# Efficient attention and a highway layer on one core: weight landing buffers, tanh to SBUF, a plain fp16 product, and a remade list of steps

## The chip, the cores and the metric

The kernel runs on one core of a Trainium2 chip. A core has a matrix engine (TensorE, in the profile PE, with its weight loads as PEld), a vector engine (VectorE, DVE), an activation engine (ScalarE, ACT), a general engine (GpSimd, POOL) and an engine that only issues DMAs and waits (SyncE, SP). Each engine works through its own instructions in order and waits for others by semaphores. SBUF is the working memory, PSUM the memory that matrix products are written to. The metric is the device time of one execution in microseconds, and lower is better.

## The reference

Two layers follow each other. The first is linear attention over batch 8, 8 heads, 576 positions and 64 channels:

```
q_s = exp(q) / sum over channels of exp(q)         (after subtracting a maximum)
k_s = exp(k) / sum over positions of exp(k)        (after subtracting a maximum)
kv  = k_s^T v           per batch and head, 64 x 64
attn = q_s kv           -> x, 4608 tokens x 512
```

The second is a highway layer over the 4608 tokens, with two 512 x 512 weights and one bias:

```
H = max(x w_h, 0);  T = sigmoid(x w_t + b_t);  out = T*H + (1 - T)*x
```

All inputs and the output are float32. Inside, the kernel works with fp16 operands and fp32 sums.

## The kernel before

The 4608 tokens are cut into 36 tiles of 128 tokens. For each pair of batches there are nine tiles: four of the first batch, four of the second, and one that holds the last 64 positions of both. Tile 35 is the last. Tiles 0 and 4 are worked in two halves of the heads.

Per batch, `ek` and `eq` take the exponentials of k and q on ACT, `vc` casts v to fp16 (on POOL, ACT or DVE, by a letter in the list of steps), `kv` multiplies k and v on PE, `kr` and `kn` (DVE) take the reciprocal of the sums and write the normalised block to `kvb`, `qt` turns q on PE through PSUM, and `qc` copies it back (DVE or ACT).

Per tile, PE computes `xu` (q times kv), DVE takes a reciprocal (`rs`) and writes the normalised x in fp16 (`x`). PE turns x (`xt`), DVE or ACT copies it out of PSUM (`xe`), and PE multiplies it by both weights: `mh` gives x w_h/2 - x/2 into a bank `gps`, `mt` gives x w_t onto the bias in a bank `tps`. The bias gets there by `bw`: a matmul on PE, or a copy of the finished bias rows `ball` by ACT. `th` takes tanh of half of `tps` (ACT), `dd` takes d = max(-x/2, gps) (DVE), `uu` makes u = (tanh + 1) d, and `oo` makes the output u + x. So the sigmoid is written with tanh, and T*(H - x) becomes (tanh + 1) times d.

There are two ways to u. In 28 of the 36 tiles (line 396), `th` writes back into `tps` and DVE reads PSUM to form (tanh + 1) d in one instruction. In 8 "lifted" tiles, `th` writes fp16 to SBUF (line 377), POOL forms d + x (`ee`, line 388) and tanh times d (`uu`, line 394), and `oo` adds these two. `oo` runs on POOL in all tiles but the last, where DVE does it in two halves.

The order of everything is written out by hand: the text `ORDER` is a list of some 700 steps, such as `xu_5_0` or `bw_7:A`, and each step issues its instructions at that place. Since every engine works in order, this list sets the order on each engine. `fill_n` issues n matmuls without use, which keep PE busy while it has nothing to do.

Loads of k, q, v and the weights and nearly all stores are issued by SP, in the order of the list; each of k, q and v has three landing buffers. The weights land in tiles of their own (`w32`) and are cast to fp16 by `wtc` and `whc`; `whd` subtracts half of an identity from the diagonal blocks of w_h. Two neighbouring tiles share one output buffer of 128 x 2 x 512 float32 (`oo` in the pool `op`, 3 buffers), which two stores of 64 rows each empty. The tiles without a mate, 8, 17, 26 and 31 to 35, have one of 128 x 512 (tag `o1`).

PSUM has two banks for `tps`, two for `gps`, and one place for turned x, which all tiles share.

The softmax here doesn't subtract the row's maximum and nothing guards it: scores larger than these inputs give would overflow.

## Time and profile before

The median of three timed runs is 126.34 us (126.02 to 127.27). The profiled execution has a span of 126.1 us, so what the profile shows stands 0.2 us below the median.

| | |
|---|---|
| span of the profiled execution | 126.1 us |
| median of the timed runs | 126.34 us |
| busy: PE, DVE, ACT, POOL | 112.1, 101.4, 92.8, 70.2 us |
| moved by DMA | 40.08 MB, on average 318 GB/s |
| DMA in the first three quarters of the span | 370 to 405 GB/s in nearly every slice |
| granted TensorE clock | 0.977 on average |
| instructions | 3549 |

A line of a group reads: source line, engine, operation, what it writes and reads with shapes, how often; then the busy time and the mean duration of one; then the time for which the engine was idle before these instructions and who ended it. Instructions that follow each other on DVE overlap by some 0.08 us, so that two 0.68 us passes take 1.28 us. A row of the timeline gives the start, the duration, the engine and the line. A row of windows gives each engine's busy time in a stretch.

### The profile page before, as it was taken

To read this page: it belongs to the slowest core of one execution; us is meant where nothing else is said; L and a number is where in the kernel's file an instruction comes from. 1 tells how busy PE (TensorE), PEld (TensorE's weight loads), DVE (VectorE), ACT (ScalarE), POOL (GpSimd) and SP (SyncE) were. 2 spreads that over 40 slices of the span, in tenths; PEclk is the share of its full clock that TensorE was granted. 3 is DMA by queue.
4 is the path that set the end of the run, shared out by engine and by line. 5 is a ranking of instruction groups with operands and counts; after the bars stand their busy time and mean duration, and the time that the engine had idled before them with its cause. 6 is when DMAs were issued, how large, how long until landed. Compare 5 with 4: busy or idle time off the path is not lost.

```text
span 126.1 us, 3549 instructions
## 1 busy us (share of the span) xinstructions
PE 112.1 (89%) x1415; PEld 68.6 (54%) x1415; DVE 101.4 (80%) x237; ACT 92.8 (74%) x144; POOL 70.2 (56%) x71
## 2 busy tenths in 40 slices
PE   5798979994999799999999999999899999999800
PEld 4485854543755365556564666557456656555400
DVE  5504769996868779999989899989889989999640
ACT  4098363995747999968959979999899996557500
POOL 5030000485304694785716769999974896786610
PEclk9999999999599999999999999999999999999996
DMA  4999999999999999999999999999987363733994
GB/s 110 376 386 373 383 385 377 387 378 387 391 394 400 396 385 300 376 394 396 405 393 391 402 404 397 393 400 394 393 324 229 86 166 83 144 70 80 222 237 127
DMA packets 20372, 40.08 MB, mean 318 GB/s; under 512 B 1282, under 2 KB 3586, under 8 KB 20356
## 3 DMA queue, kind: packets, MB, share of 16 engines
q1 hardware_dynamic: 20192, 39.72, 90.1%
q8 instruction: 11, 0.18, 0.6%
q10 hardware_dynamic: 164, 0.14, 0.4%
q14 instruction: 5, 0.04, 0.1%
HBM read 30.41 MB, written 9.44 MB: 316 GB/s over the span
## 4 chain that ended last, share of the span: by engine, by line
PE 36%; DMA 22%; DVE 12%; POOL 9%; ACT 7%; SPq 5%; issue 3%; DVEq 0%; POOLq 0%; ACTq 0%
PE gps L363 11%; DMA q<-in_q_dram 9%; PE tps L357 9%; DMA w32h<-in_moe_w_h_dram 7%; POOL o L412 6%; DMA out_dram<-o 5%; PE xu L312 5%; PE qps L286 4%; DVE u L396 4%; PE turned L334 3%; DVE d L383 2%; ACT qe L276 2%; ACT ek L232 2%; PE kv L248 2%; PE turned L168 2%
## 5 line engine op out<-in xcount | busy, mean ns | idle before, releaser
L412 POOL TENSOR_TENSOR o<-u,x 128x512 f32<-128x512 f16 x27 | 31.2, 1155 | 33.2 <-DVE u L396 32.7
L363 PE MATMUL gps<-w16h,xT 128*128 128x512 f16 x144 | 36.9, 384 | 0.0
L357 PE MATMUL tps<-w16t,xT 128*128 128x512 f16 (+1 forms) x148 | 36.8, 373 | 0.0
L327 DVE TENSOR_TENSOR x<-xu,rs 128x512 f16<-128x512 f32 (+1 forms) x38 | 24.9, 659 | 1.2
L383 DVE SCALAR_TENSOR_TENSOR d<-x,gps 128x512 f16<-128x512 f16 x36 | 24.3, 679 | 1.0 <-PE gps L363 0.8
L379 ACT ACTIVATE tps<-tps 128x512 f32<-128x512 f32 (+1 forms) x29 | 16.4, 568 | 11.0 <-PE tps L357 9.6
L276 ACT ACTIVATE qe<-q 128x1024 f16<-128x1024 f32 (+1 forms) x24 | 19.8, 845 | 3.0 <-DMA q<-in_q_dram 3.0
L396 DVE SCALAR_TENSOR_TENSOR u<-tps,d 128x512 f16<-128x512 f32 (+1 forms) x29 | 19.3, 669 | 3.1 <-POOL o L412 1.4
L357 PEld LDWEIGHTS <-xT 128*128 128x128 f16 x148 | 13.6, 98 | 11.6
L363 PEld LDWEIGHTS <-xT 128*128 128x128 f16 x144 | 13.2, 99 | 11.9 <-issue 0.5
L232 ACT ACTIVATE ek<-k 128x1152 f16<-128x1152 f32 (+1 forms) x20 | 18.8, 966 | 0.2 <-DMA k<-in_k_dram 0.2
L347 ACT COPY tps<-ball 128x512 f32<-128x512 f32 x27 | 15.9, 594 | 3.4 <-DVE u L396 3.4
L238 POOL CAST v<-v 128x1152 f16<-128x1152 f32 (+1 forms) x11 | 10.6, 969 | 10.8 <-DMA v<-in_v_dram 9.6
L312 PE MATMUL xu<-kvb,eq 128*128 128x130 f16 (+1 forms) x160 | 15.0, 229 | 1.4 <-DVE kvb L266 1.2
L334 PE MATMUL turned<-idh,x 128*128 128x128 f16 x144 | 14.4, 222 | 0.2 <-ACT xT L341 0.2
L168 PE MATMUL turned<-blank 128*128 128x256 f16 x88 | 12.4, 295 | 2.2 <-POOL blank L147 1.3
L312 PEld LDWEIGHTS <-eq 128*128 128x128 f16 (+1 forms) x160 | 10.3, 103 | 6.1 <-DVE kvb L266 1.7
L286 PE MATMUL qps<-idh,qe 128*128 128x128 f16 x144 | 12.3, 222 | 1.3 <-ACT qe L276 1.2
L334 PEld LDWEIGHTS <-x 128*128 128x128 f16 x144 | 9.8, 99 | 6.0 <-DVE x L327 2.7
L286 PEld LDWEIGHTS <-qe 128*128 128x128 f16 x144 | 9.5, 99 | 5.5 <-ACT qe L276 2.5
L168 PEld LDWEIGHTS <-blank 128*128 128x128 f16 x88 | 9.0, 106 | 4.1 <-POOL blank L147 1.3
L394 POOL TENSOR_TENSOR u<-th,d 128x512 f16<-128x512 f16 x8 | 9.2, 1155 | 2.8 <-ACT th L377 1.3
(45 smaller groups left out, 111.4 us busy)
## 6 DMA issues: line engine op xcount, KB each, us to landing
out_dram<-o SPq DMA_DIRECT2D x28, 256.0 KB, 9.6
v<-in_v_dram SPq DMA_DIRECT2D x6, 1152.0 KB, 13.5
k<-in_k_dram SPq DMA_DIRECT2D x6, 1152.0 KB, 13.9
q<-in_q_dram SPq DMA_DIRECT2D x6, 1152.0 KB, 14.0
k<-in_k_dram SPq DMA_DIRECT2D x4, 576.0 KB, 9.4
v<-in_v_dram SPq DMA_DIRECT2D x4, 576.0 KB, 6.6
out_dram<-o SPq DMA_DIRECT2D x14, 128.0 KB, 3.0
q<-in_q_dram SPq DMA_DIRECT2D x2, 640.0 KB, 11.4
```

Source lines behind the costliest of these rows:

```text
L168: nc.tensor.matmul(spare, blank[:, 0:P], blank[:, 0:2 * P], start=True, stop=True, skip_group_check=True)
L232: nc.scalar.activation(t[:, :, c:c + n].rearrange("p j c d -> p c j d"), T[f"k32{b}"][:, c:c + n].rearrange("p c (j d) -> p c j d", j=NJ), ...
L276: nc.scalar.activation(t[:, j0:j1].rearrange("p j c d -> p c j d"), T[f"q32{b}"].rearrange("p c (j d) -> p c j d", j=NJ)[:, :, j0:j1], AF.Exp)
L286: nc.tensor.matmul(t[:, (j - j0) // 2, 2 * kk:2 * kk + 2, (j - j0) % 2], T[f"qe{b}"][:, j, 2 * kk:2 * kk + 2].rearrange("p c d -> p (c d)" ...
L312: nc.tensor.matmul(dst, T[f"eq{b}_{jp // 2}"][:, jp % 2, n], kvb[b % NKV][:, hh, kk], start=True, stop=True, skip_group_check=True)
L327: nc.vector.tensor_mul(t[:, k0:k1], sums(i, k)[:, :, :, 0:64], T[f"rs{i}_{k}"][:, 0:k1 - k0].unsqueeze(3).to_broadcast([P, k1 - k0, 4, D]))
L334: nc.tensor.matmul(t[:, n], T[f"x{i}"][:, n * P:(n + 1) * P], idh, is_transpose=True, start=True, stop=True, skip_group_check=True)
L357: nc.tensor.matmul(T[f"tps{i}"][:, cs], T[f"xT{i}"][:, n], w16["t"][:, n, cs], start=False, stop=(n == 3), skip_group_check=True)
L363: nc.tensor.matmul(t, T[f"xT{i}"][:, n], w16["h"][:, n], start=(n == 0), stop=(n == 3), skip_group_check=True)
L383: nc.vector.scalar_tensor_tensor(t, T[f"x{i}"], -0.5, T[f"gps{i}"], op0=ALU.mult, op1=ALU.max)
L396: nc.vector.scalar_tensor_tensor(t[:, cs], T[f"tps{i}"][:, cs], 1.0, T[f"d{i}"][:, cs], op0=ALU.add, op1=ALU.mult)
L412: eng.tensor_add(t[:, cs], T[f"u{i}"][:, cs], T[f"{'e' if lifted(i) else 'x'}{i}"][:, cs])
```

## The change

- The tiles `w32` are gone. Each half of a weight lands in a buffer of the output pool, which now has seven buffers. One half of w_t is cast by ACT, the other by POOL, where DVE cast both.
- 33 tiles are lifted where 8 were. In these, tanh goes to SBUF as fp16 and u is a plain fp16 product of two SBUF tiles: on DVE in 16 tiles (`uu_..:T`), on POOL in 17 (`:P`). Of their 33 sums d + x, 12 are on DVE (`ee_..:D`) and 21 on POOL. Tiles 5, 28 and 35 still form u from PSUM.
- 10 of the output sums of whole tiles, and one half of the last tile's, are on DVE (`oo_..:D`), the rest on POOL, the last tile's other half among them.
- The last tile's two column halves have a PSUM bank each, the second from the pool of `qt`; its first product is of half 1, then half 0.
- The halves of tiles 0 and 4 may come in either order in `mt` and `mh`.
- A tile that holds rows of two batches, and the last one, is stored by one DMA where two were used. 13 stores are issued by ACT (`st_..:A`).
- The list of steps is new throughout: the order of loads (the weights come after q of batch 0), which copies are on which engine, where stores are issued, and 116 filling matmuls where 88 were.

Per engine the list moves these counts: copies of turned x on DVE from 22 to 17 and on ACT from 16 to 21; casts of v on ACT from 8 to 3, on DVE from 1 to 6, on POOL 11 as before; copies of turned q on ACT from 10 to 8; the bias by PE in 9 tiles before, in 8 and a half after.

```diff
--- before
+++ after
@@ ORDER @@
-b_0 b_32 setuppool fill_16 setupdve k_0_0 v_0_0 v_0_2 k_0_2 q_0_0 w_h_0 q_0_4 bsplit w_h_2 fill_4 bp w_t_0 bc vc_0_0:A
-w_t_2 bw_0:A ek_0_1 vc_0_2 k_1_0 ek_0_0 vc_0_3 vc_0_1:A ek_0_3 fill_30 kv_0_0 q_1_0 ek_0_2 kr_0_0 kn_0_0 fill_5 kv_0_1
-eq_0_0 v_1_0 kr_0_1 kn_0_1 fill_6 qt_0_0 whc_0 k_1_2 qc_0_0 half fill_9 xu_1_0 xu_0_1 xu_0_0 eq_0_1 rs_0_1 rs_1_0
-v_1_2 rs_0_0 x_1_0 bw_1:A x_0_0 fill_10 qt_0_1 x_0_1 whd_0 qc_0_1:A q_1_4 fill_2 xt_0_1 whc_2 xt_0_0 whd_1 whd_3
-xe_0_1 fill_6 xu_2_0 whd_2 xe_0_0 xt_1_0 rs_2_0 mh_0_0 v_2_0 xe_1_0 x_2_0 mh_0_1 eq_0_2 wtc_0:D mh_1_0 wtc_2:D mt_0_0
-dd_1 mt_0_1 dd_0 xu_3_0 th_0_0 xt_2_0 mt_1_0 rs_3_0 k_2_0 xe_2_0:D ek_1_0 uu_0_0 mh_2_0 th_1_0 x_3_0 eq_1_0 bw_2
...
-st_30_0_1 st_32_0_1 oo_33_0 th_34_0 mt_35_0 uu_34_0 st_33_0_0 mt_35_1 st_28_0_1 dd_35 th_35_0 oo_34_0 st_33_0_1
-th_35_1 uu_35_1 uu_35_0 st_34_0_0 oo_35_1 oo_35_0:P st_34_0_1 st_35_1_1 st_35_1_0 st_35_0_1 st_35_0_0
+setupdve v_0_2 k_0_0 q_0_0 k_0_2 b_0 ek_0_0 b_32 vc_0_3:A v_0_0 setuppool eq_0_0 ek_0_2 fill_20 bsplit vc_0_1:D ek_0_3
+q_0_4 w_t_0 fill_30 fill_30 half vc_0_2 vc_0_0 qt_0_0 w_h_0 ek_0_1 fill_20 kv_0_0 k_1_0 qc_0_0 w_t_2 kv_0_1 kr_0_0 w_h_2
+v_1_0 bp kn_0_0 eq_0_1 qt_0_1 q_1_0 xu_0_0 bc kr_0_1 kn_0_1 k_1_2 xu_0_1 wtc_0 rs_0_1 wtc_2:P xu_1_0 rs_1_0 qc_0_1:A
+rs_0_0 x_0_1 fill_16 v_1_2 whc_0 x_0_0 xt_0_1 x_1_0 vc_1_1 xe_0_1:D bw_0 whd_1 vc_1_0 xt_0_0 xe_0_0 xu_3_0 xt_1_0 rs_3_0
+xe_1_0 whd_0 bw_1 q_1_4 k_2_0 x_3_0 ek_1_1 whc_2 mt_0_0 xu_2_0 eq_0_2 mh_0_0 v_2_0 xt_3_0 mt_0_1 whd_2 rs_2_0 th_0_0
+mt_1_0 vc_1_2 q_2_0 whd_3 ek_1_0 mh_0_1 eq_1_0 th_1_0 xe_3_0:D mh_3_0 x_2_0 xt_2_0 kv_1_0 dd_0 kr_1_0 xe_2_0:D uu_0_0:T
+ek_1_2 dd_3 ek_1_3 vc_1_3:A mh_1_0 bw_2 mt_2_0 qt_1_0 dd_1 ee_0:D kn_1_0 oo_0_0:D bw_3 mh_2_0 th_2_0 kv_1_1 uu_1_0:P
+dd_2 kr_1_1 ee_3 mt_3_0 qc_1_0:A xu_4_0 eq_1_2 kn_1_1 qt_1_2 eq_1_1 ee_1:D qc_1_2 xu_5_0 th_3_0 rs_5_0 xu_4_1 bw_4
+qt_1_1 rs_4_0 x_5_0 qc_1_1 x_4_0 k_3_0 rs_4_1 xt_5_0 bw_5 qt_0_2 ee_2 xu_6_0 xe_5_0 x_4_1 xt_4_0 rs_6_0 v_3_0 ek_2_2
+uu_3_0:T x_6_0 mt_5_0 xt_4_1 oo_1_0 q_3_0 mh_5_0 xe_4_0:D xe_4_1:D xu_7_0 qc_0_2 rs_7_0 xt_6_0 mt_4_1 v_4_0 xe_6_0
+mt_4_0 oo_3_0 k_4_0 uu_2_0:T mh_4_1 th_5_0 mh_4_0 oo_2_0 vc_2_2 th_4_0 x_7_0 dd_5 vc_2_0:D ek_2_0 xu_8_0 bw_6 eq_2_0
+rs_8_0 xt_7_0 x_8_0 xe_7_0 dd_4 uu_5_0 mh_6_0 uu_4_0:P eq_2_1 kv_2_0 dd_6 mt_6_0 kr_2_0 th_6_0 qt_2_0 q_4_0 ee_4 mh_7_0
...
+xt_34_0 st_30_0_0 dd_33 uu_32_0:P bw_34:A oo_32_0 st_25_0_0:A ee_31:D oo_31_0 mt_33_0 xe_34_0 xt_35_0 st_32_0_1:A
+th_33_0 ee_33:D mh_34_0 uu_33_0:T mt_34_0 bw_35_0:A oo_33_0 dd_34 st_32_0_0 xe_35_0 ee_34:D mh_35_0 bw_35_1 th_34_0
+st_30_0_1 mt_35_1 st_28_0_0 st_31_0_0 st_31_0_1 st_23_0_0:A uu_34_0:T mt_35_0 st_33_0_0 dd_35 th_35_1 oo_34_0 st_33_0_1
+th_35_0 uu_35_1 st_34_0_1:A uu_35_0 oo_35_0:D st_34_0_0 oo_35_1 st_35_1_0 st_35_0_0:A
@@ -93,7 +94,7 @@
     xp = pool("xp", 6)
     xtp = pool("xtp", 3)
     dp = pool("dp", 3)
-    op = pool("op", 3)
+    op = pool("op", 7)
     PS = bass.MemoryType.PSUM
     ps_t = pool("ps_t", 2, space=PS)
     ps_g = pool("ps_g", 2, space=PS)
@@ -105,7 +106,6 @@
     idf = consts.tile([P, P], FP32, name="idf")
     idh = consts.tile([P, P], FP16, name="idh")
     half = consts.tile([P, P], FP32, name="half")
-    w32 = {w: consts.tile([P, KC, DM], FP32, name="w32" + w) for w in "th"}
     w16 = {w: consts.tile([P, KC, DM], FP16, name="w16" + w) for w in "th"}
     b32 = consts.tile([P, DM], FP32, name="b32")
     b16 = consts.tile([P, DM], FP16, name="b16")
@@ -139,8 +139,13 @@
     def halves(b, k):
         return (k, k + 1) if b < 2 else (0, 2)
 
+    PIECES = (0, 256, 512)
+
     def columns(i, h):
-        return slice(h * DM // 2, (h + 1) * DM // 2) if i == LAST else slice(0, DM)
+        return slice(PIECES[h], PIECES[h + 1]) if i == LAST else slice(0, DM)
+
+    def gate(i, h):
+        return f"tps{i}_{h}" if i == LAST else f"tps{i}"
 
 
     def setup_pool(e):
@@ -190,7 +195,8 @@
 
     def load_w(e, w, c):
         src = dict(t=moe_w_t, h=moe_w_h)[w]
-        nc.sync.dma_start(w32[w][:, c:c + 2], src.rearrange("(c p) n -> p c n", p=P)[:, c:c + 2])
+        T[f"w{w}{c}"] = op.tile([P, 2, DM], FP32, tag="o32", name=f"w32{w}_{c}")
+        nc.sync.dma_start(T[f"w{w}{c}"], src.rearrange("(c p) n -> p c n", p=P)[:, c:c + 2])
 
     def load_b(e, r):
         nc.scalar.dma_start(b32[r:r + 1], moe_b_t.rearrange("(o n) -> o n", o=1))
@@ -198,17 +204,18 @@
 
     def wt_cast(e, c):
         if e == "D":
-            nc.vector.tensor_scalar_mul(w16["t"][:, c:c + 2], w32["t"][:, c:c + 2], 1.0)
-        else:
-            nc.scalar.copy(w16["t"][:, c:c + 2], w32["t"][:, c:c + 2])
+            nc.vector.tensor_scalar_mul(w16["t"][:, c:c + 2], T[f"wt{c}"], 1.0)
+        else:
+            copy = nc.gpsimd.tensor_copy if e == "P" else nc.scalar.copy
+            copy(w16["t"][:, c:c + 2], T[f"wt{c}"])
 
     def wh_cast(e, c):
-        nc.vector.tensor_scalar_mul(w16["h"][:, c:c + 2], w32["h"][:, c:c + 2], 0.5)
+        nc.vector.tensor_scalar_mul(w16["h"][:, c:c + 2], T[f"wh{c}"], 0.5)
 
     def wh_diag(e, c):
         cs = slice(c * P, (c + 1) * P)
         nc.vector.scalar_tensor_tensor(
-            w16["h"][:, c, cs], w32["h"][:, c, cs], 0.5, half, op0=ALU.mult, op1=ALU.subtract)
+            w16["h"][:, c, cs], T[f"wh{c // 2 * 2}"][:, c % 2, cs], 0.5, half, op0=ALU.mult, op1=ALU.subtract)
 
     def bsplit(e):
         for r in (0, 32):
@@ -341,37 +348,43 @@
         copy(t[:, 2 * k0:2 * k1], T[f"xtps{i}"][:, 2 * k0:2 * k1])
 
 
-    def bw(e, i):
-        t = T[f"tps{i}"] = ps_t.tile([P, DM], FP32, tag="tps", name=f"tps_{i}")
+    def bw(e, i, h=0):
+        bank = (ps_t, "tps") if i < LAST or h == 0 else (ps_q, "qps")
+        t = T[gate(i, h)] = bank[0].tile([P, DM], FP32, tag=bank[1], name=f"tps_{i}_{h}")
+        cs = columns(i, h)
         if e == "A":
-            nc.scalar.copy(t, ball)
-        else:
-            nc.tensor.matmul(t, ones, b16, start=True, stop=False, skip_group_check=True)
+            nc.scalar.copy(t[:, cs], ball[:, cs])
+        else:
+            nc.tensor.matmul(t[:, cs], ones, b16[:, cs], start=True, stop=False, skip_group_check=True)
 
     def parts_of(i, k):
         return range(2 * k, 2 * k + 2) if i in HALVED else range(4)
 
     def mt(e, i, k):
         cs = columns(i, k)
-        for n in parts_of(i, k):
-            nc.tensor.matmul(T[f"tps{i}"][:, cs], T[f"xT{i}"][:, n], w16["t"][:, n, cs], start=False,
-                             stop=(n == 3), skip_group_check=True)
+        parts = parts_of(i, k)
+        first = once(f"mt{i}", lambda: k) == k and len(parts) < 4
+        for n in parts:
+            nc.tensor.matmul(T[gate(i, k)][:, cs], T[f"xT{i}"][:, n], w16["t"][:, n, cs], start=False,
+                             stop=(n == parts[-1] and not first), skip_group_check=True)
 
     def mh(e, i, k):
+        first = f"gps{i}" not in T
         t = once(f"gps{i}", lambda: ps_g.tile([P, DM], FP32, tag="gps", name=f"gps_{i}"))
-        for n in parts_of(i, k):
-            nc.tensor.matmul(t, T[f"xT{i}"][:, n], w16["h"][:, n], start=(n == 0), stop=(n == 3),
-                             skip_group_check=True)
-
-
-    LIFTED = {s.split(":")[0] for s in ORDER.split() if s.startswith("uu") and s.endswith(":P")}
+        parts = parts_of(i, k)
+        for n in parts:
+            nc.tensor.matmul(t, T[f"xT{i}"][:, n], w16["h"][:, n], start=(first and n == parts[0]),
+                             stop=(n == parts[-1] and not (first and len(parts) < 4)), skip_group_check=True)
+
+
+    LIFTED = {s.split(":")[0] for s in ORDER.split() if s.startswith("uu") and s[-2:] in (":P", ":T")}
 
     def lifted(i):
         return f"uu_{i}_0" in LIFTED
 
     def th(e, i, h):
         cs = columns(i, h)
-        src = T[f"tps{i}"][:, cs]
+        src = T[gate(i, h)][:, cs]
         if lifted(i):
             T[f"th{i}"] = dp.tile([P, DM], FP16, tag="th16", name=f"th16_{i}")
             nc.scalar.activation(T[f"th{i}"], src, AF.Tanh, scale=0.5)
@@ -385,15 +398,17 @@
     def ee(e, i):
         if lifted(i):
             T[f"e{i}"] = dp.tile([P, DM], FP16, tag="e16", name=f"e16_{i}")
-            nc.gpsimd.tensor_add(T[f"e{i}"], T[f"d{i}"], T[f"x{i}"])
+            eng = nc.vector if e == "D" else nc.gpsimd
+            eng.tensor_add(T[f"e{i}"], T[f"d{i}"], T[f"x{i}"])
 
     def uu(e, i, h):
         cs = columns(i, h)
         t = once(f"u{i}", lambda: dp.tile([P, DM], FP16, tag="u16", name=f"u16_{i}"))
         if lifted(i):
-            nc.gpsimd.tensor_mul(t, T[f"th{i}"], T[f"d{i}"])
-        else:
-            nc.vector.scalar_tensor_tensor(t[:, cs], T[f"tps{i}"][:, cs], 1.0, T[f"d{i}"][:, cs],
+            eng = nc.vector if e == "T" else nc.gpsimd
+            eng.tensor_mul(t, T[f"th{i}"], T[f"d{i}"])
+        else:
+            nc.vector.scalar_tensor_tensor(t[:, cs], T[gate(i, h)][:, cs], 1.0, T[f"d{i}"][:, cs],
                                            op0=ALU.add, op1=ALU.mult)
 
 
@@ -403,26 +418,27 @@
     def oo(e, i, h):
         cs = columns(i, h)
         if mate(i) is None:
-            t = once(f"o{i}", lambda: op.tile([P, DM], FP32, tag="o1", name=f"o32_{i}"))
+            t = once(f"o{i}", lambda: op.tile([P, DM], FP32, tag="o1", bufs=3, name=f"o32_{i}"))
         else:
             a = min(i, mate(i))
             both = once(f"oo{a}", lambda: op.tile([P, 2, DM], FP32, tag="o32", name=f"o32_{a}"))
             t = both[:, i - a]
-        eng = nc.vector if e == "D" or i == LAST else nc.gpsimd
+        eng = nc.vector if e == "D" else nc.gpsimd
         eng.tensor_add(t[:, cs], T[f"u{i}"][:, cs], T[f"{'e' if lifted(i) else 'x'}{i}"][:, cs])
 
     def st(e, i, h, r):
         bs, jp = tiles[i]
         b = bs[r % len(bs)]
         cs, rows = columns(i, h), slice(NP * r, NP * r + NP)
-        eng = nc.scalar if i == LAST and r else nc.sync
+        eng = nc.scalar if e == "A" else nc.sync
         dst = out[b * S:(b + 1) * S, cs].rearrange("(p j) n -> p j n", j=NJ)
         if mate(i) is not None:
             eng.dma_start(dst[:, 2 * jp + r - 2:2 * jp + r + 1:2], T[f"oo{i - 1}"][rows])
         elif len(bs) == 1:
             eng.dma_start(dst[:, 2 * jp + r], T[f"o{i}"][rows, cs])
         else:
-            eng.dma_start(dst[:, 8], T[f"o{i}"][rows, cs])
+            ends = out[b * S:(b + 2) * S, cs].rearrange("(r j) n -> r j n", j=NJ)
+            eng.dma_start(ends[:, 8], T[f"o{i}"][:, cs])
 
     does = dict(
         setuppool=setup_pool, setupdve=setup_dve, half=half_of_identity, bsplit=bsplit, fill=fill,
```

## The prediction

> **What bounds the kernel now.** I read the page first, then windows, waits, timeline and groups.
>
> ```profile
> span 126.1 us, 3549 instructions
> ...
> PE 112.1 (89%) x1415; PEld 68.6 (54%) x1415; DVE 101.4 (80%) x237; ACT 92.8 (74%) x144; POOL 70.2 (56%) x71
> ...
> L412 POOL TENSOR_TENSOR o<-u,x 128x512 f32<-128x512 f16 x27 | 31.2, 1155 | 33.2 <-DVE u L396 32.7
> ```
>
> PE is the busiest, and POOL alone has room. The page averages over stages, so I cut the span where the first matrix product of batch 1 starts (33.7) and where the products end.
>
> ```profile
> 0.00:18.00 18.00, 14.48 (x186) 11.14 (x187) 9.53 (x38) 9.82 (x14) 2.87 (x11) 1.00 0.93 333
> 18.00:33.70 15.70, 13.52 (x167) 8.33 (x166) 13.26 (x31) 10.83 (x18) 6.98 (x7) 0.93 1.06 383
> 33.70:119.30 85.60, 84.12 (x1067) 49.11 (x1064) 76.89 (x165) 71.42 (x111) 59.51 (x53) 0.99 0.90 313
> ```
>
> The columns after the length are PE, PEld, DVE, ACT and POOL. In the long stage PE is busy 84.1 of 85.6 us, and it is truly full: in the timeline four 512-column products follow each other at 0.86 us, 0.216 each, four of `xu` take 0.23 and four turns 0.22. A tile needs 8 x 0.216 + 0.23 + 0.22 + 0.22 and 0.16 of `kv`, 2.56 us; 32 tiles need 82 us. DVE is close behind with 76.9 (90%). Before this stage PE waits:
>
> ```profile
> 28.21 0.67 POOL L238 CAST v<-v 128x576 f16<-128x576 f32 x1
> ...
> 30.99 0.41 PE L312 MATMUL xu<-kvb,eq 128*128 128x130 f16 x4 [1.19 <-DVE kvb L266]
> ```
>
> The last product of tiles 0 to 3 starts at 27.4, the first of batch 1 at 33.7. POOL casts v at 28.21 because an output sum held it from 27.11; `kv` starts at 28.93 and DVE ends its four passes on the result at 30.94. The end is another chain:
>
> ```profile
> 118.18 1.04 PE L357 MATMUL tps<-w16t,xT 128*128 128x256 f16 x8
> ...
> 119.32 0.77 ACT L379 ACTIVATE tps<-tps 128x256 f32<-128x256 f32 x2 [1.21 <-PE tps L357]
> ...
> 122.36 1.20 SPq L425 DMA_DIRECT2D out_dram<-o  x2
> ```
>
> From 119.2 to the end are 6.9 us; SP issues stores without a pause from 116.2 to 123.6, 0.6 us each.
>
> **The head.** The order of loads changes, but v's second half of batch 1 stays the 15th load with the same bytes ahead; in the trace its neighbours land at 25.25 and 28.52, so it lands at about 26.9. POOL then has only casts in front: cast 26.9 to 27.6, `kv` to 28.2, `kr`, `kn` (0.17 + 0.59) to 29.0, `ee_1`, `qc_1_2` and reciprocals to 29.9, `x_5` to 30.5, turn and copy 0.8, product at 31.4 instead of 33.7: **2.3 us gained**. Behind POOL's early wait stand `uu_1` and sums, which PE doesn't need. w_h's second half moves from 15.9 to about 20.7 (one q and one k load more ahead at 1.5 us each, and part of w_t); tiles 0 to 3 then finish at about 28.3, still before 31.4, so it costs nothing unless it slips 3 us. The 28 more `fill` matmuls (0.11 us each, 3 us) end before w_t's second half can be cast at about 20.4: hidden. Casting w_t on ACT and POOL (1.05 each by the 1024-element rows) frees 1.3 us of DVE. The half clock in the middle row (0.93 of 15.7 us) I leave, as PE's pause has about the same length.
>
> **The tail.** Only one half is left after the last product: tanh 0.37, product 0.42, sum 0.42, one issue 0.6, landing 2.0 (from 123.0 to 125.0 before), closing 1.1: 5.0 with gaps, **1.9 us gained**. The other half's sum on POOL, about 0.6, lies beside it. Fewer stores (one DMA for two) and 13 issued by ACT take SP's row of issues away. On ACT they cost 13 x 0.6 = 8 us, and the instructions behind them wait: `xe_17`, `xe_34`, the last tanh. ACT loses five v casts (5.2) and gains five copies (2.9) and a weight cast (1.1), and so ends near 98 us: below PE.
>
> **Parts worth little.** The waits say so:
>
> ```profile
> ACT tps L347 <- DVE u L396: 3.4, 6, 0.8
> ...
> PEld L286 <- ACT qe L276: 2.5, 3, 1.3
> ...
> POOL o L412 <- DMA out_dram<-o: 0.4, 2, 0.2
> ```
>
> Tanh to SBUF frees the PSUM bank earlier, but only ACT waited for that, 3.4 us, and PE stayed full. Seven buffers replace three where POOL waited 0.4 us. Loads get ahead of stores, and PE waited under 1 us for the last q. Together 0 to 1 us.
>
> **DVE, passes counted.** A full 128x512 pass (0.68) costs 0.60 in a row, a copy of turned x 0.40. Gone: 25 u from PSUM (15.0), five copies (2.0), the weight casts (1.3), one half sum (0.3). Added: 10 full output sums (6.0), five v casts at 0.68 (3.4; the 1024-element cast row, 690 ns), and 28 products and sums of two fp16 SBUF tiles at a price p. That is -9.2 + 28p. No row shows p; the nearest are DVE's fp16 copy out of PSUM (mean 413 ns), its plain passes (0.68), and what POOL takes:
>
> ```profile
> L238 POOL CAST v<-v 128x1152 f16<-128x1152 f32 x7 | 8.0, 1143 | 4.7 <-DMA v<-in_v_dram 3.5 <-PE qps L286 1.2
> ...
> L238 POOL CAST v<-v 128x576 f16<-128x576 f32 x4 | 2.6, 664 | 6.1 <-DMA v<-in_v_dram 6.1
> ```
>
> Low end: the fp16 copy, 0.34 in a row; then DVE stays at its 101.4. Middle: the plain pass, 0.60; then 7 us more. High end: such a pass also waits for POOL. In this trace every pass that DVE runs beside POOL has at most one SBUF tensor of full size, and every pass with two (o, e, u) is on POOL or runs while POOL is idle. The change puts 28 + 10 with two SBUF tensors on DVE, beside a POOL that is busier still. POOL's rows say what it is short of: its casts cost 0.83 ns per column (1143 - 664 over 576), its two-tensor passes 1155 for 512, 1.9 ns per column after the same fixed part. [...]
>
> Price of that: POOL in the long stage has about 60 passes at 1.11 (their spacing at 74.66, 75.77, 76.88) and 6 casts, 74 us, some 80% of the stage. A DVE pass meets it with that chance and waits half a pass: 0.8 x 0.55 = 0.44. Of DVE's passes in the stage 25 fp16, 9 output sums and 5 casts are exposed: 39 x 0.44 = 17 us. By the same list DVE's stage is 76.9 us at p = 0.34, so 94; at 97% use (its best 6 us are 98%) 97 us from 31.0, and 5 us of tail: 133. From the other side, if the waits pack perfectly, POOL's 74 and the 17 us of DVE's exposed passes add to 91, from 31, and 4.5 after: 127. I take **130**.
>
> [...]
>
> **Rivals.** (1) *Nothing new is paid*, p = 0.34: PE decides, 31.4 + 82 + 2 us of its present waits + 5.0 = 120.5. For it: DVE at 76.9 of 84 is as full as now. Against it: two engines above 90% in fixed order. (2) *The plain pass*, p = 0.60: DVE's stage is 83.4, at 97% 86, from 31.0, then 5.0: 122.5. (3) *Waits half as long*: 39 x 0.2 gives DVE 84.7, 87.3, 31.0 and 5: 123.5 to 127, about no change. The turn between faster and slower lies at 0.27 us per exposed pass. (4) The list's stores on ACT or its new order stall PE where no buffer shows it: within 127.
>
> **How the numbers follow.** Span and timed median differ by 0.2 us; I leave that inside. Waits on POOL's reads (127 to 135, centre 130): 0.52. No price (119 to 122.5): 0.28. Plain pass (122 to 125): 0.12. Between (125 to 127.6, the 1% about 126.3 that a measurement of this kernel can hardly tell from no change): 0.08. So faster 0.40, same 0.08, slower 0.52; the likeliest case alone spans 127 to 135. The range for all runs from 120 to 133.5: it leaves out about 0.08 at either end.
>
> **What the next profile would show.** For my case: DVE rows of the fp16 product and of `ee` with means far above 0.42, or POOL passes above 1155; DVE above 93% in the long stage and PE with gaps in its products ended by DVE x or xT. Against it: these rows at 0.4 and POOL's still at 1155, PE as full as now. Head: first product of batch 1 at about 31.4. Tail: about 5 us from the last product to the end. I am wrong if DVE and POOL read side by side, or if the list keeps them apart.

## The result, and the profile after

The changed kernel takes 137.19 us (median of 4 runs, 136.74 to 137.51), the kernel before on the same chip 126.21 (126.02 to 127.27). The ratio is 1.0859, with a 95% interval from 1.0804 to 1.0914: the change makes the kernel 8.6% slower. The prediction was 130.0, slower, with a range of 120 to 133.5. Its side and its mechanism hold; its size does not.

The page of the changed kernel begins so:

```profile
span 135.1 us, 3623 instructions
...
PE 115.1 (85%) x1443; PEld 70.5 (52%) x1443; DVE 116.3 (86%) x249; ACT 93.5 (69%) x144; POOL 92.2 (68%) x85
...
DVE  5107589699999999999999999999999999999961
...
DVE 34%; POOL 12%; issue 7%; PE 5%; DMA 2%; SPq 1%; ACT 0%; DVEq 0%; POOLq 0%
```

DVE's row of slices stands at 9 from the ninth slice to the last but two, and in the chain that ended last DVE has 34% and PE 5%; in the kernel before it was DVE 12% and PE 36%. The bound has moved from PE to DVE. Cut at the same places as before (first product of batch 1, last product), with the columns PE, PEld, DVE, ACT and POOL:

```profile
18.00:35.17 17.17, 15.36 (x187) 9.13 (x186) 15.72 (x39) 10.58 (x19) 8.05 (x8) 1.00 1.06 383
35.17:127.51 92.34, 83.37 (x1058) 47.96 (x1057) 90.19 (x177) 73.72 (x115) 78.76 (x64) 1.00 0.85 283
127.51:135.10 7.59, 0.27 (x3) 0.00 (x0) 3.25 (x6) 0.61 (x2) 2.18 (x3) 0.77 0.69 190
```

Against the profiled execution of before, the head is 1.4 us longer (its first product of batch 1 came at 33.73), the long stage 7.1 (from 33.73 to 118.95 it was 85.2, with DVE at 76.5 and PE at 83.8) and the tail 0.4 (7.15). In the long stage DVE is now busy for 90.2 of 92.3 us, 98%; PE has 83.4 us of work, about as before, and waits the rest of the time. What it waits for is x:

```profile
PEld L341 <- DVE x L334: 6.3, 8, 1.7
PEld L319 <- DVE x L334: 5.2, 9, 1.2
...
PE turned L341 <- DVE x L334: 3.9, 4, 1.6
```

The first number is the sum of the waits, the last the longest. In the kernel before, the row of the turns (`PEld L334 <- DVE x L327`) stands at 2.7 us, the longest 0.5. Where DVE's time goes is seen in the groups, shapes kept apart:

```profile
L409 DVE TENSOR_TENSOR u<-th,d 128x512 f16<-128x512 f16 x16 | 12.4, 772 | 0.0
...
L402 DVE TENSOR_TENSOR e<-d,x 128x512 f16<-128x512 f16 x12 | 9.2, 772 | 0.2
...
L427 DVE TENSOR_TENSOR o<-u,e 128x512 f32<-128x512 f16 x8 | 7.5, 935 | 0.0
...
L245 DVE CAST v<-v 128x1152 f16<-128x1152 f32 x5 | 6.3, 1261 | 0.0
...
L396 DVE SCALAR_TENSOR_TENSOR d<-x,gps 128x512 f16<-128x512 f16 x36 | 24.1, 677 | 0.9 <-PE gps L376 0.5
```

The four kinds of pass that the change puts on DVE have means far above what the shortest of them take (about 0.4 for u and e); the pass `d`, with one operand in PSUM, has kept its 0.68. POOL's two-tensor rows went from about 1155 to 1202 (o), 1253 (e) and 1315 (u). In the timeline (start, duration, engine) each of these DVE passes starts 0.1 us behind one of POOL and ends only some 0.3 us after it:

```profile
118.98 1.16 POOL L427 TENSOR_TENSOR o<-u,e 128x512 f32<-128x512 f16 x1
119.08 1.34 DVE L409 TENSOR_TENSOR u<-th,d 128x512 f16<-128x512 f16 x1
120.22 1.21 POOL L409 TENSOR_TENSOR u<-th,d 128x512 f16<-128x512 f16 x1
120.34 1.37 DVE L402 TENSOR_TENSOR e<-d,x 128x512 f16<-128x512 f16 x1
```

The wait can be followed pass by pass. Of the 43 passes of these four kinds (16 u, 12 e, 10 o, 5 v), 28 start while POOL is in a two-tensor pass or a cast: they are longer than the pass alone (0.42, 0.42, 0.69 and 0.76 us, measured below) by 0.53 us in the mean and by at most 0.98. The other 15 are not longer at all.

A time stands 1.7 to 1.8 us above its execution's span in every run of this study. The executions of the kernel before are of two kinds, 125.2 to 126.4 us of span at a mean clock of 0.975 to 0.980 and 123.9 to 125.1 at 0.984 to 0.993, and the profiled one is of the first kind: its granted clock is 0.55 in the mean from 31.2 to 35.0 us, after PE's gap of 1.19 us. Where that stretch lies almost wholly ahead of the long stage or is missing, in two runs with the old list below, the stage takes 84.1 us; against that it has lost 8.3.

### The profile page after: what moved, and what is told of

Its sections match the earlier page's. It is cut to its first block, busy times and chain, and to the rows that moved or that the text cites. A ratio compares the mean times of both kernels' runs of the same rounds, so it can differ in the third digit from the quotient of the medians.

```text
span 135.1 us, 3623 instructions
## 1 busy us (share of the span) xinstructions
PE 115.1 (85%) x1443; PEld 70.5 (52%) x1443; DVE 116.3 (86%) x249; ACT 93.5 (69%) x144; POOL 92.2 (68%) x85
## 2 busy tenths in 40 slices
DMA packets 20293, 40.08 MB, mean 297 GB/s; under 512 B 1202, under 2 KB 3506, under 8 KB 20276
## 4 chain that ended last, share of the span: by engine, by line
DVE 34%; POOL 12%; issue 7%; PE 5%; DMA 2%; SPq 1%; ACT 0%; DVEq 0%; POOLq 0%
DVE x L334 9%; DVE d L396 6%; DVE u L409 4%; POOL o L427 4%; POOL e L402 3%; DVE e L402 3%; DVE o L427 3%; DVE v L245 3%; POOL u L409 3%; DMA out_dram<-o 2%; POOL v L245 2%; DVE eq L302 2%; DVE rs L328 2%; PE tps L368 1%; PE gps L376 1%
## 5 line engine op out<-in xcount | busy, mean ns | idle before, releaser
L427 POOL TENSOR_TENSOR o<-u,e 128x512 f32<-128x512 f16 x25 | 30.0, 1202 | 8.5 <-DVE u L409 4.7
L402 POOL TENSOR_TENSOR e<-d,x 128x512 f16<-128x512 f16 x21 | 26.3, 1253 | 5.8 <-DVE rz L267 3.3
L334 DVE TENSOR_TENSOR x<-xu,rs 128x512 f16<-128x512 f32 (+1 forms) x38 | 24.9, 658 | 0.7
L390 ACT ACTIVATE th<-tps 128x512 f16<-128x512 f32 x33 | 19.5, 595 | 6.4 <-PE tps L368 4.5
L409 POOL TENSOR_TENSOR u<-th,d 128x512 f16<-128x512 f16 x17 | 22.3, 1315 | 2.2 <-DVE d L396 1.2
L348 ACT COPY xT<-turned 128x512 f16<-128x512 f16 (+1 forms) x21 | 12.0, 574 | 15.5 <-PE turned L341 13.7
L245 POOL CAST v<-v 128x1152 f16<-128x1152 f32 (+1 forms) x11 | 12.0, 1092 | 13.1 <-DMA v<-in_v_dram 13.1
L173 PE MATMUL turned<-blank 128*128 128x256 f16 x116 | 15.1, 296 | 1.3 <-POOL blank L152 1.3
L356 ACT COPY tps<-ball 128x512 f32<-128x512 f32 (+1 forms) x28 | 15.9, 586 | 0.3
L319 PEld LDWEIGHTS <-eq 128*128 128x128 f16 (+1 forms) x160 | 9.6, 100 | 9.6 <-DVE x L334 5.2
L173 PEld LDWEIGHTS <-blank 128*128 128x128 f16 x116 | 12.2, 106 | 3.5 <-POOL blank L152 1.3
```

Of the source, the lines that this page charges most:

```text
L173: nc.tensor.matmul(spare, blank[:, 0:P], blank[:, 0:2 * P], start=True, stop=True, skip_group_check=True)
L319: nc.tensor.matmul(dst, T[f"eq{b}_{jp // 2}"][:, jp % 2, n], kvb[b % NKV][:, hh, kk], start=True, stop=True, skip_group_check=True)
L334: nc.vector.tensor_mul(t[:, k0:k1], sums(i, k)[:, :, :, 0:64], T[f"rs{i}_{k}"][:, 0:k1 - k0].unsqueeze(3).to_broadcast([P, k1 - k0, 4, D]))
L390: nc.scalar.activation(T[f"th{i}"], src, AF.Tanh, scale=0.5)
L402: eng.tensor_add(T[f"e{i}"], T[f"d{i}"], T[f"x{i}"])
L409: eng.tensor_mul(t, T[f"th{i}"], T[f"d{i}"])
```

## Experiments

**Theory.** A DVE pass that reads two tensors from SBUF and a POOL pass exclude each other. The new passes wait for POOL, this fills DVE, and a full DVE lets PE wait for x. **Rivals.** The number of passes on DVE, at any price; the new list of steps by itself; the weights in the output buffers; the late loads and the fills for the head; the stores for the tail.

The runs were taken in three groups, each with the kernel before beside it (medians 126.45, 127.26 and 126.37 us); a ratio is to the kernel before of its own group.

### The price by itself

Not the kernel, but rows of passes, each kind alone and then two kinds side by side:

```diff
+PHASES = [
+    ("product", 12, "", 0), ("sum32", 12, "", 0), ("onepsum", 12, "", 0), ("psumcopy", 12, "", 0), ("cast", 6, "", 0),
+    ("", 0, "sum", 8), ("", 0, "sum32", 8), ("", 0, "cast", 8),
+    ("product", 12, "sum", 12), ("sum32", 12, "sum", 12), ("onepsum", 16, "sum", 10), ("psumcopy", 24, "sum", 10),
+    ("cast", 8, "sum", 8), ("product", 10, "cast", 10)]
```

> Not the kernel at all (nothing of the reference is computed): rows of passes on DVE and POOL, each kind alone and then side by side. Theory: alone the fp16 product of two SBUF tiles takes 0.41, the sum with fp32 output 0.65, the pass with one operand in PSUM 0.68, the fp16 copy out of PSUM 0.41; POOL's sum 1.15. Side by side, the product and the sum with two SBUF tiles take turns with POOL's passes, so that a pair lasts 1.4 to 1.6 us from start to start and the DVE row's mean is above 1; the passes with an operand in PSUM stay as alone, and so does POOL beside them. [...] Rival, shared bandwidth: both kinds get longer together by a common factor, also those with a PSUM operand. Rival, no contention: all rows as alone.

The groups of this run, window by window: first alone (product, sum with fp32 output, pass with a PSUM operand, copy out of PSUM, cast; then POOL's sum), then side by side (products, sums, passes with a PSUM operand between POOL's row and the casts).

```profile
L61 DVE TENSOR_TENSOR u<-th,d 128x512 f16<-128x512 f16 x11 | 4.7, 425 | 0.4
L62 DVE TENSOR_TENSOR o<-th,d 128x512 f32<-128x512 f16 x11 | 7.6, 693 | 0.4
L63 DVE SCALAR_TENSOR_TENSOR dx<-x,g 128x512 f16<-128x512 f16 x11 | 7.6, 686 | 0.4
L79 DVE CAST v<-v 128x1152 f16<-128x1152 f32 x1 | 0.8, 759 | 0.6 <-DMA v<-in_v_dram 0.6
L68 POOL TENSOR_TENSOR p<-pa,x 128x512 f32<-128x512 f16 x8 | 9.2, 1150 | 0.5
...
L61 DVE TENSOR_TENSOR u<-th,d 128x512 f16<-128x512 f16 x12 | 15.1, 1256 | 0.4
L62 DVE TENSOR_TENSOR o<-th,d 128x512 f32<-128x512 f16 x12 | 18.3, 1523 | 0.4
L67 POOL TENSOR_TENSOR e<-pa,x 128x512 f16<-128x512 f16 x10 | 11.5, 1151 | 0.7
L63 DVE SCALAR_TENSOR_TENSOR dx<-x,g 128x512 f16<-128x512 f16 x16 | 11.0, 686 | 0.5
L65 DVE CAST v<-v 128x1152 f16<-128x1152 f32 x8 | 12.7, 1592 | 0.2
```

Beside POOL the product takes 1.26 us instead of 0.43, the sum 1.52 instead of 0.69, and the cast from SBUF to SBUF, which has one source, 1.59 instead of 0.76. The pass with one operand in PSUM stays at 0.686, and POOL beside it at 1.151; the copy out of PSUM stays at 0.42 too. So it is turns and not shared bandwidth, and the cast of v belongs to those who pay. In each of the three the excess is the same 0.83, though their own times differ.

### The 38 passes without what they read: a failed try

In the changed kernel the 16 products, the 12 sums `e` and the 10 output sums on DVE become copies of an unused block in PSUM.

```diff
+    still = turned[:, 1].rearrange("p c d -> p (c d)")
...
-            eng.tensor_mul(t, T[f"th{i}"], T[f"d{i}"])
+            if e == "T":
+                nc.vector.tensor_copy(t, still)
+            else:
+                nc.gpsimd.tensor_mul(t, T[f"th{i}"], T[f"d{i}"])
```

> The changed kernel, in which DVE's 16 fp16 products u, its 12 sums e and its 10 full output sums are each replaced by one copy of an unused 128x512 fp16 block in PSUM into the same destination (those products and sums are left out; POOL's part, all loads, stores and matrix products stay). The nearest row is the copy of turned x out of PSUM, 406 ns, which kept that time beside POOL. Theory (a DVE pass with two SBUF tensors and a POOL pass exclude each other): the 38 passes lose some 12.5 us of waiting, DVE in the long stage falls from 90.2 to about 78, POOL's sums go back to about 1.16, PE decides again, and the span falls from 135.1 to 126 to 129 us (the head and the tail keep their losses), timed 128 to 130.5. Rival, that the number of DVE passes and their places in the list make the loss, and not what they read: the same number of passes in the same places, so 134 to 137.

136.98 us (136.59 to 137.06), ratio to the kernel before 1.0802 (1.0743 to 1.0861): the time of the changed kernel, as the rival had it. But the groups and the waits say something else:

```profile
L412 DVE COPY u<-turned 128x512 f16<-128x512 f16 x16 | 6.7, 417 | 2.7 <-PE turned L342 1.8 <-ACT xT L349 0.8
...
L405 POOL TENSOR_TENSOR e<-d,x 128x512 f16<-128x512 f16 x21 | 24.2, 1155 | 7.9 <-DVE d L397 7.7
```

```profile
ACT xT L349 <- DVE e L403: 6.6, 3, 2.3
...
PE turned L342 <- DVE o L432: 1.7, 4, 0.6
```

The price is gone (417 ns, POOL's `e` at 1155 again), and DVE's long stage fell to 80.6 us of a stage of 94.2. But the unused block lies in the tile `turned`, into which PE turns x, and the semaphores now order PE's turns, ACT's copies and DVE's copies among each other. The experiment put a new wait in the place of the old one and settles nothing about the time.

### The same with fills

The same 38 passes become fills with a constant, which read nothing. A fill takes 485 ns, so 38 cost 18.4 us; what they replace would cost 28 x 0.42 + 10 x 0.69 = 18.7 if it did not wait.

```diff
-            eng.tensor_mul(t, T[f"th{i}"], T[f"d{i}"])
+            if e == "T":
+                nc.vector.memset(t, 0.25)
+            else:
+                nc.gpsimd.tensor_mul(t, T[f"th{i}"], T[f"d{i}"])
```

> The changed kernel again with its 38 DVE passes over two SBUF tensors left out (16 products u, 12 sums e, 10 output sums), but now each is a fill of the same destination with a constant, which reads nothing and so brings no new dependence; in the copies out of PSUM it was seen that PE's turns of x and these copies waited for each other, since they lie in one PSUM tile. A fill of 128x512 took 485 ns, fp16 or fp32, in the rows of passes measured alone. Theory (waiting for POOL): DVE's long stage falls from 90.2 to about 78, PE is busy all through it, the stage lasts 85 to 87.5 us where it took 92.3, span 128 to 130.5, timed 129.5 to 132.5. Rival, that the new list holds PE up by itself, whatever DVE's passes cost: the stage stays above 90, timed 135 to 137. A fill that waits for POOL too would show as a row mean above 0.55; then the run says little.

129.85 us (129.15 to 131.17), ratio 1.021 (1.0104 to 1.0316). Its groups and its long stage:

```profile
L404 POOL TENSOR_TENSOR e<-d,x 128x512 f16<-128x512 f16 x21 | 24.3, 1155 | 4.0 <-DVE rz L267 3.0 <-DVE d L396 0.9
...
L411 DVE MEMSET u<- 128x512 f16 x16 | 7.8, 485 | 0.9
...
L245 DVE CAST v<-v 128x1152 f16<-128x1152 f32 x5 | 5.4, 1071 | 0.0
```

```profile
34.94:119.36 84.42, 83.34 (x1059) 48.17 (x1057) 79.84 (x179) 73.19 (x115) 74.39 (x64) 1.00 0.91 309
```

The time and DVE's stage are as expected, the stage a little shorter. It goes from 92.3 to 84.4 us, PE is busy for 83.3 of it, and DVE falls to 79.8. The places in the list, the number of passes and their price alone are the same as in the changed kernel; what is taken away is reading, and with it the waiting (the fills also drop their waits for tanh and d, but in the changed kernel DVE idled 0.0 and 0.2 us ahead of these groups). So the waits make nearly the stage's whole loss: 84.4 us stand against 84.1 with the old list, and the new list by itself costs the stage next to nothing. What is left of the 2.1% is the head (its first product of batch 1 comes at 34.94) and the tail (8.0 us).

### The old list in the changed code, and 24 such passes in it

`old_list` keeps of the change the seven buffers with the weights in them, the last tile's two banks and the single stores; the order, the lifted tiles and the engines are those of the kernel before.

> The changed kernel's code with the list of steps of the kernel before (28 tiles with u out of PSUM, all output sums on POOL, no store on ACT), so that of the change there remain the seven output buffers in which the weights land, the last tile's halves in banks of their own with half 1 first and half 0's sum on DVE and the other's on POOL, and one store where a tile holds rows of two batches. Theory: nothing of this costs anything; the tail gains 1 to 2 us and the long stage stays at 85 us, so 124 to 126 us against 126.2. Rival, that the weights in the output pool or the banks cost something: 127 or more, with PE waiting in the head for weights.

125.92 us (125.65 to 127.19), ratio 0.9955 (0.9913 to 0.9998): at the upper end of what was expected, half a percent at most. The long stage is 84.1 us and the tail 6.8. Buffers, banks and stores cost nothing, and bring little.

`old_list_24` adds to it, in 12 tiles, one product and one sum of two SBUF tensors on DVE, with POOL's passes as they were:

```diff
-uu_7_0
+uu_7_0:T ee_7:D
 (the same for tiles 10, 12, 13, 16, 18, 19, 23, 24, 25, 27 and 29)
```

> The same as old_list, but in 12 tiles of the middle (7, 10, 12, 13, 16, 18, 19, 23, 24, 25, 27, 29) tanh goes to SBUF, and DVE makes u as a product of two fp16 SBUF tiles and e as their sum with x, in the place where it made u out of PSUM; POOL's passes stay the same in number. Alone, a tile costs DVE 2 x 0.41 - 0.60 = 0.2 more, 2.6 in all. Theory: each of the 24 passes waits 0.38 in the mean, 9 us, so DVE's long stage rises from 76.5 to about 88 of then 89 us, the rows of both have means near 0.75, and the time is 3 to 6 us above old_list. Rival, no waiting: rows at 0.41, DVE at 79 of 85, within 0.7 us of old_list, or faster since the bank of tps comes free earlier.

129.84 us (129.29 to 130.91), ratio 1.0255 (1.0181 to 1.033), 3.9 above `old_list`. Its groups:

```profile
L409 DVE TENSOR_TENSOR u<-th,d 128x512 f16<-128x512 f16 x12 | 7.5, 624 | 1.0 <-ACT th L390 0.9
L402 DVE TENSOR_TENSOR e<-d,x 128x512 f16<-128x512 f16 x12 | 6.9, 574 | 0.0
```

The loss is in the expected window, and the rival's rows at 0.41 are not there. But the means are 0.62 and 0.57 where 0.75 was expected: 4.3 us of waiting instead of 9. POOL is busy here for 59.3 of 87.9 us, where it was 78.8 of 92.3. But its busy share is not the chance of a meeting: 8 of the 24 passes start during a pass of POOL, and those wait 0.54 in the mean, the others not at all. Where the list places a pass decides whether it pays. DVE stands at 81.0 of 87.9 and not at its limit, so the time also goes to waits of x in the fixed order: PE's weight loads wait 5.3 us for x ahead of a turn, against 2.4 in `old_list`.

### Giving the passes back: two tries

In `no_two_sbuf` the 16 tiles form u from PSUM again, POOL takes over the output sums and the four sums `e` of DVE that are left, and ACT the casts.

```diff
-uu_3_0:T ... ee_10:D ... oo_5_0:D ... vc_2_0:D
+uu_3_0 (ahead of the bias that takes its bank) ... oo_5_0 ... vc_2_0:A
```

> The changed kernel with these parts undone, everything else as it is: the 16 tiles whose u was a fp16 product on DVE form u from PSUM again (their sums e fall away, and where the next bias needs the bank, u stands before it), the other 4 sums e of DVE and its 9 whole output sums in the remaining places go to POOL, and 5 casts of v go from DVE to ACT. So DVE has no pass with two SBUF tensors but the last tile's half. Theory: DVE's stage falls from 90.2 to about 76 us, POOL's stays near 78, and the stage comes to 85 to 88 us: span 127 to 131, timed 129 to 133. Rival, the list: 135 or more, with PE waiting for other things than DVE's x.

138.11 us (137.52 to 138.71), ratio 1.0863 (1.0765 to 1.0962). DVE is down to 70.7 of 93.3 us and POOL's rows are at 1155 to 1158, but now the bank decides:

```profile
ACT tps L356 <- DVE u L411: 7.9, 7, 2.2
...
DVE u L411 <- ACT tps L392: 6.8, 7, 2.5
```

In the second try the bias is moved behind u instead, and 4 of the tiles form u on POOL.

> A second try at the changed kernel without DVE passes over two SBUF tensors, since in the first try u was moved up in the list and DVE then waited for tanh, and ACT's next bias for u: now 12 of the 16 tiles form u from PSUM in the place where u stands, with the bias of the tile that takes the bank moved behind it; the other 4 form u on POOL; the remaining sums e and the output sums of DVE are on POOL and the 5 casts of v on ACT, as before. DVE's stage then needs some 72 us and POOL's some 83. Theory: 129 to 133, since no engine is above 90%. Rival (the new list needs the bank to be free right after tanh): ACT waits for u and PE for the bias, 134 to 138, as in the first try.

141.72 us (140.7 to 142.63), ratio 1.1188 (1.111 to 1.1266): worse. DVE waits for tanh 7.0 us, ACT for u 7.7, and POOL, now at 87.2 of 99.9 us, is late with a cast of v that the product of k and v waits for. Both misses say the same: the new list is built on a bank that is free right after tanh, and its DVE passes could not be taken back in these two ways. They say nothing about the price.

### The head

`head_old` has the first part of the old list, up to the last step of kv of batch 1, and then the new one.

> The changed kernel with the first part of the old list, up to the last normalising of kv of batch 1 (loads, fills, casts, tiles 0 to 3 with u out of PSUM), and the rest of the new list as it stands. Theory: the head's loss comes from the new list's first part alone (bias load late behind an exponential on ACT, 116 fills, casts of the weights beside POOL), so the first product of batch 1 comes at 33 to 34.5 instead of 35.2, and the time falls by 0.7 to 2.2, to 135 to 136.5. Rival, that the long stage swallows it (it is bound by DVE's passes, which are the same): no change within 0.5.

135.34 us (135.3 to 135.65), ratio 1.0666 (1.059 to 1.0743): 1.85 below the changed kernel's median, and 1.2 in the profiled spans (133.9 and 135.1). The first product of batch 1 comes at 33.72, and the long stage, 92.5 us with DVE at 89.9, is the same. The head's loss stands by itself and adds to the stage's.

`fewer_fills` takes 36 fills out of the new head, and `b_and_fills` puts the bias loads first as well.

```diff
-b_0 ek_0_0 b_32 ... ek_0_1 fill_20 kv_0_0 ... x_0_1 fill_16 v_1_2
+(b_0 b_32 first, in b_and_fills alone) ... ek_0_1 kv_0_0 ... x_0_1 v_1_2
```

> The changed kernel without two of its rows of fills: the 20 that stand on PE ahead of the first product of k and v, and the 16 ahead of the first turn of x. In its trace the 20 end at 14.79, while the two casts of v that this product needs end at 12.0 and 13.3, and the 16 run from 17.58 to 19.49 where the first x is ready at 18.5. Theory (the head's loss is made by PE's fills): the first product of k and v comes at 13.4 instead of 14.7, the first x is turned a microsecond earlier, the first product with a weight stands at 20 or earlier (21.4), and the first of batch 1 comes 0.5 to 1.4 us earlier than 35.2; timed 135.7 to 136.7. Rival, the weights: the second half of w_t is cast at 20 to 21 whatever PE does, and nothing is gained after it: within 0.4 of 137.2. A half clock after the missing fills would eat the gain; the granted clock tells.

> The same as fewer_fills, and in addition the two loads of the bias stand first on ACT's queue, as in the kernel before, so that DVE no longer waits 7.1 us for them with a cast of v behind. Theory: that cast ends near 11.5 instead of 13.3, the first product of k and v starts at 12.2, when PE has ended its earlier fills and turns, and the head gains another 0.5 to 1 us over fewer_fills: first product of batch 1 at 33.2 to 34.2, timed 134.8 to 136. Rival, that v's load of batch 1 sets the head (it lands at 27 in either kernel): nothing beyond fewer_fills.

In the timeline of the changed kernel the bias holds DVE until 12.5 with a cast of v behind it, and the fills hold PE until 14.8, so that the first product of k and v starts at 14.71:

```profile
11.05 0.42 DVE L222 CAST b<-b 1x512 f16<-1x512 f32 x1 [7.09 <-DMA b<-in_moe_b_t_dram]
...
12.44 2.35 PE L173 MATMUL turned<-blank 128*128 128x256 f16 x20
12.57 0.75 DVE L245 CAST v<-v 128x576 f16<-128x576 f32 x1
...
14.71 0.78 PE L255 MATMUL kv<-v,ek 64*64 64x65 f16 x72
```

Without the fills it starts at 12.27, but the first product of batch 1 gains only 0.5 (34.66); with the bias first as well it comes at 34.01. The times are 136.24 (135.94 to 136.78; ratio 1.0759, 1.0687 to 1.083) and 136.51 (135.73 to 137.49; 1.0783, 1.0713 to 1.0852). The second kernel's time misses its window, as three of its four runs have a granted clock of 0.968 to 0.975 against 0.985 in the best one, which took 135.73. Taking fills and late bias away gives back 1.16 of the head's 1.4 us. How much of it is the bias is not shown: with the bias first, the first product of k and v comes at 13.39 and not at the expected 12.2, while in `fewer_fills` PE waits 0.81 and 2.00 us ahead of its turns of x and behind that works at about half the speed: two products of 512 columns take 1.06 us at 20.32 where they take 0.59 in `b_and_fills`, whose granted clock is 1.00 from 18 to 34 us (in the mean of the profiled executions 0.974 and 0.985). So the fills that were in the way may also have kept the clock up.

The rest stands behind kv, and there the head pays the stage's price. In the changed kernel the sum `e` of tile 1 lies between the normalised kv and x of batch 1:

```profile
31.19 0.59 DVE L273 TENSOR_TENSOR kvb<-kv,rz 64x128 f16<-64x128 f32 x2
31.82 0.95 DVE L402 TENSOR_TENSOR e<-d,x 128x512 f16<-128x512 f16 x1
```

From the start of that normalising to the start of x it takes 2.05 us (x at 33.24). In `head_old`, which has no such sum there, it takes 1.39 (30.36 to 31.75). That is 0.66 of the 1.45 us between the two heads.

### The tail

> The changed kernel with six buffers instead of three for the output of tiles without a mate, so that tile 35's sums don't wait until tile 32's store has landed. Theory: both sums of the last tile start as soon as u is there, 1.2 to 1.4 us earlier; the stores then wait for nothing but SP and ACT issuing them; timed 1 to 1.8 us less than 137.2. Rival, that the stores' queue sets the end: the last store is issued after the others anyway, and the gain is under 0.4.

```diff
-t = once(f"o{i}", lambda: op.tile([P, DM], FP32, tag="o1", bufs=3, name=f"o32_{i}"))
+t = once(f"o{i}", lambda: op.tile([P, DM], FP32, tag="o1", bufs=6, name=f"o32_{i}"))
```

137.73 us (137.01 to 137.95), ratio 1.0839 (1.0755 to 1.0923): no gain. Changed kernel, then this one, each with the last tile's sums and last store:

```profile
131.16 0.67 POOL L427 TENSOR_TENSOR o<-u,x 128x256 f32<-128x256 f16 x1 [1.38 <-DMA out_dram<-o]
131.19 0.92 DVE L427 TENSOR_TENSOR o<-u,x 128x256 f32<-128x256 f16 x1 [1.21 <-DMA out_dram<-o]
...
132.14 0.38 ACTq L441 DMA_DIRECT2D out_dram<-o  x1
```

```profile
130.37 0.67 POOL L427 TENSOR_TENSOR o<-u,x 128x256 f32<-128x256 f16 x1
...
130.65 0.66 DVE L427 TENSOR_TENSOR o<-u,x 128x256 f32<-128x256 f16 x1
...
131.53 0.52 SPq L441 DMA_DIRECT2D out_dram<-o  x1
```

The waits are gone and the sums run 1.2 to 1.4 us earlier (from the last product, which is 0.63 later here). But from the last issue to the end it takes 135.9 - 132.05 = 3.85 us where it took 135.1 - 132.52 = 2.58: SP's six stores of 128 KB, the last store at 131.53 among them, land after 3.3 us in the median, where the one issued at 132.14 landed after 1.9. The DMA rows of the last 10 us, 0.25 us per digit, of the changed kernel and of this one, suggest why:

```profile
DMA  9966987789899999988668898988845997000000
```

```profile
DMA  9878876988999999997679889889999730000000
...
DMA packets 1314, 2.01 MB, mean 201 GB/s; under 512 B 208, under 2 KB 464, under 8 KB 1313
```

The DMA engines are busy at 60 to 100% in nearly every slice until about 134, with 2.0 MB of stores that are late (2.09 MB in the changed kernel). An earlier last store then stands behind them; no run takes these stores away, so that their drain sets the end is argued and not shown.

The last kernel, `best`, is `old_list` with six such buffers, one late store on ACT, and 15 fills in PE's two gaps before batch 1.

> The kernel old_list (the old list in the changed code: seven buffers, the last tile's own banks, one store for two), and in addition six buffers for the tiles without a mate, the last but one tile's second store on ACT, and 15 fills in PE's two gaps before the first products of batch 1 (0.77 us ahead of the second half of batch 1's product of k and v, 1.19 us ahead of its first xu), where about half of the executions of the kernel before and of old_list show a half clock afterwards. Theory: no execution has the half clock any more (0.6 us in the median), and the tail loses its wait for a landing store, 0.5 us: 124.5 to 125.5 against 126.4 of the kernel before. Rival: the fills delay the products by what they save, and SP's row of stores sets the end: 125.5 to 126.2.

126.64 us (126.33 to 127.11), ratio 1.0002 (0.997 to 1.0033). This is above both windows. The clock is between 0.981 and 0.993 in all 12 runs, the first product of batch 1 comes at 33.47 and the last product at 117.53, a microsecond before that of `old_list`, whose profiled execution had a clock of 0.978; and then the tail takes 7.58 us instead of 6.77. The issue of its last store ends a microsecond earlier than in `old_list` (121.09 and 122.13) and its span only 0.2 us earlier (125.1 and 125.3): again the gain is given back behind the last issue. No kernel of this study beats the one before by more than the half percent of `old_list`.

## Why the prediction was right or wrong

**The mechanism: right.** The predicted marks are there: rows of u and e at 772 where 0.42 is the price alone, POOL's passes above 1155, DVE at 98% of the stage, PE's gaps ended by x. With two SBUF inputs the product took 1.26 instead of 0.43 beside POOL, while a pass with one operand in PSUM kept its 0.686. The cast of v, which the prediction counted among the exposed passes, pays too (1.59 for 0.76). What makes the two engines take turns no run shows; that they do is measured, and a product in the rows waits 0.83 behind a POOL pass of 1.15, not the whole of it.

**The price at rest: right.** The product took 0.42 alone and the low end was taken for the sum, 0.34 in a row; in the tail of the changed kernel one that meets nobody starts at 128.08 and the next pass at 128.42.

**The price of a wait: 0.44 predicted, 0.34 measured.** Against 0.42, 0.69 and 0.76 alone, the groups after have an excess of 5.6 (u), 4.2 (e), 2.4 (o) and 2.5 us (v), 14.7 over 43 passes. In the long stage it is 13.8 us over 38 passes, where the prediction had 17 over 39. The prediction took POOL's busy share, 0.8, as the chance of a meeting and half of POOL's pass, 0.55, as the wait. Measured, 28 of 43 passes meet POOL, 0.65, and these wait 0.53: the wait was nearly right and the chance too high. That chance is not a rule either: in `old_list_24`, where POOL is busy for 67% of the stage, a third of the passes meet it and 0.18 is paid per pass. So a price so near the predicted one is partly luck.

**The long stage: 94 in the middle of the sum (91 to 97), 92.3 measured.** Right. DVE's own sum was 94 too and came to 90.2, mostly by the 3 us of waits that were not there, and DVE is as full (98%) as the 97% assumed.

**The head: 2.3 us gained was predicted, 1.4 were lost.** This is the step that failed most: the sum that brings the first product of batch 1 to 31.4, where it came at 35.17. The load of v and its cast were right (POOL's cast at 27.32, predicted 26.9). But the sentence that tiles 0 to 3 "finish at about 28.3, still before 31.4, so it costs nothing" failed, and with it that the fills are hidden: the first product with a weight came at 21.44 instead of 19.30, the last of tiles 0 to 3 ended at about 31.2, and on PE, which works in order, the second half of kv stood behind these products:

```profile
27.32 0.67 POOL L245 CAST v<-v 128x576 f16<-128x576 f32 x1 [3.12 <-DMA v<-in_v_dram]
...
28.93 1.03 PE L376 MATMUL gps<-w16h,xT 128*128 128x512 f16 x4
29.89 0.48 PE L255 MATMUL kv<-v,ek 64*64 64x65 f16 x36
```

Its cast was ready at 28.0 and it ran at 29.89, 1.7 us after the predicted end of kv, 28.2. Then the prediction gave 0.9 us to `ee_1`, a copy and the reciprocals; they took 1.4, since `ee_1` waited for POOL, a price that the prediction counted in the stage alone. It followed the loads and looked for cover at the weights' casts, but not at the bias, of whose two loads ACT issues the second behind an exponential, nor at which products stand ahead of kv on PE.

**The tail: 5.0 predicted, 7.6 measured.** The sum of the last half's steps left out two things. DVE has a backlog (d of tile 35 starts at 128.42, 0.9 us after the last product began, since e and u of earlier tiles stand ahead), and the output buffers of the tiles without a mate are only three, so the sums wait 1.2 to 1.4 us for a store to land. The second turned out not to be the bound: with the wait removed the end stays, most likely because of the stores' drain. Nor did fewer stores "take SP's row of issues away": SP still issues five in a row from 126.39 to 130.68. What the end of this tail hangs on stays open.

**Outside the span: 0.2 predicted, 1.8 measured.** The profiled execution of before had the half clock (0.55 for 3.8 us), and so its span stood near the median of the timed runs by chance. The sentence "I leave that inside" hid 1.6 us.

Together, from the 31.0 at which the sum lets DVE's stage begin: head 31.0 to 35.2 is 4.2 more, the stage 1.7 less, the tail 2.6 more, outside 1.8 more, in all 6.9 of the 7.2 us between 130.0 and 137.19. The range reached 133.5, as it took in uncertain waits, but no bound for a head or a tail that loses.

**Rivals.** "Nothing new is paid" and "the plain pass" fall with the rows (the sum of the latter, 31.0, 86 and 5.0, is 122.0 and not 122.5; nothing hangs on it). "Waits half as long" (0.2) falls with 0.34. "The list's stores or its order stall PE": in the stage no (84.4 us with the waits taken out), in the head yes.
